# Even shares of FFN pieces, single GpSimd products and stores on SyncE in an RWKV and SwiGLU kernel

## The chip, the cores and the metric

The kernel runs on one core of one Trainium2 chip. The metric is the device time of one execution in microseconds (us), lower being better. The kernel before took 592.2 us (the median of 3 runs, 592.04 to 593.37). A core has five engines, each with an instruction queue of its own that it works through in order: TensorE (PE in the profile, PEld its weight loads), VectorE (DVE), ScalarE (ACT), GpSimd (POOL) and SyncE (SP, which here only starts DMAs; ACT starts some too). Waits between engines go by semaphores.

## The reference

An attention layer (RWKV-5) with 4 batches, 8 heads, 768 positions and head width 48 is followed by a SwiGLU feed-forward block (FFN) over the 3072 rows that it gives:

```python
# per batch and head; w in 0.85 to 0.95, u small
for t in range(S):
    cur = outer(u * k[t], v[t])
    y[t] = r[t] @ (state + cur)
    state = w[:, None] * state + outer(k[t], v[t])
x = y.transpose(0, 2, 1, 3).reshape(B * S, H * D)      # 3072 x 384
g, val = x @ w_gate, x @ w_val                         # 384 x 1536 each
out = (g / (1 + exp(-g)) * val) @ w_out                # 1536 x 384
```

All is 32-bit floating point, apart from the weights, which come as 64-bit numbers and are rounded in the kernel.

## The kernel before, in words

**Attention in 24 steps.** The sequence is cut into 24 blocks of 128 rows; step `s` of the main loop (`for s in range(4, N + 2)`; steps 0 to 3 are written out before it, the head) prepares block `s + 1`, makes the scores of block `s - 1` and the outputs of block `s - 2`. From block 12 (`PAIRED`) a block is two halves of 64 rows from two batches. Per block GpSimd makes four products of 128x384: `scale_k` (k times a table of powers of w, L353), `scale_r` (r likewise, L356), and in `own_product` `own_begin` (r times k, L264) and `own_end` (times u, L267). DVE sums the last by rows at the start of the step of that block (`own_sum`, L275); ACT makes eight diagonals from the sums (`diagonal`, L376, through the queue `small`). SP moves the scaled products in blocks (`move_blocks`, L435, eight DMAs), DVE transposes them in the next step (`turn_blocks`, L456). `paired_scores` lets TensorE make the scores (L523) and, beside them, the state update of the block before (L571). What DVE does with both goes into the queue `lazy`: four masked copies (L531) and four state adds (L587), and with the second add of each half GpSimd multiplies the state by w^64 (L590, with the table `w64`). Before the next scores are made, what is left in `lazy` is flushed.

**The FFN in pieces.** The gate, value and output matmuls are cut into pieces, closures in the list `todo`. `queue(g)` adds them at odd steps: 24 gate pieces for the first pair of blocks, then groups of 41, 40 and 40 pieces at steps 9, 13 and 17, and 13 at step 21. A group has projection pieces (`two_projections`, L740), and 26 pieces of `three_beside`, which hold 60 rounds of matmuls: a round is four instructions of L924. A fast algorithm for 3x3 blocks is used there, for which GpSimd adds up weight tiles (`w_forms`, L854, nine per group of fifteen rounds) and, in the first of these groups alone, weights in place (`in_place`, L827); DVE and ACT add up results out of PSUM (L948) and ACT and DVE make the activation (L955, L948).

**The order.** All is written out by hand. `gaps(s, n)` is called at five places of a step (n = 0 to 4) and takes pieces from `todo` by `feed`. Each piece that is fed takes one item of `lazy` along, and up to three of `small`. At n = 0 a step computes its share of pieces, which is spread over the five gaps; one of gap 1's is fed inside `turn_blocks`. Up to step 17 the share empties `todo` by the step before the next group comes (at most 14 pieces a step); from step 18 it divides what is queued, and 14 to come, by the steps left:

```python
if s < 18:
    share[0] = min(-(-len(todo) // (4 - (s - 9) % 4)), 14)
else:
    share[0] = -(-(len(todo) + (14 if s < 21 else 0)) // max(25 - s, 1))
```

At the start of a step `scale_k`, `scale_r` and `own_product` of the next block are issued one after the other, then the loads of block `s + 3`. In even steps from 10 on (`late`), `scale_r` and the loads come later, behind gap 1.

**The tail.** After step 25 the last eight blocks go through `three_units` (60 rounds, L924) and `project_thirds` (the output matmuls, L1153), twice. `store` (L1118) starts the DMAs of the finished rows: on ACT, but in the second of the two projections, for the first block of each pair, on SP. A block is two pieces of 64 rows, so two DMAs. In the first of the two projections that is eight DMAs on ACT, in the second four on each queue.

**w^64.** GpSimd raises w to the 64th power by six products of 128x4 (L1421) in step 9; ACT copies each half of the partitions into `w64` (L1426) and SP sends it to the other half (L1427). The head makes on DVE a table `pw` with w^(128 - x) in column x.

Of the kernel before, what the change touches and what calls it, by code (L numbers as in the profile page):

```python
# [22 lines left out]
def fast(  # L23
# [112 lines left out]
    def pieces_of(i):  # L136

        if i < PAIRED:
            c, b = divmod(i, B)
            return [(slice(0, P), b, P * c)]  # L140
        return [(slice(64 * p, 64 * p + 64), *part(i, p)) for p in range(2)]
# [127 lines left out]
    def own_product(i):  # L269
        own_begin(i)  # L270
        own_end(i)
# [83 lines left out]
    def scale_r(i):  # L355
        pool.tensor_mul(rhat_of(i)[:, :, 0:D], raw(i)[1], rscale)  # L356
# [6 lines left out]
    def keep_natural_tables():  # L363
        for bank, dst in zip(banks, (kscale, rscale)):
            act.copy(dst, bank[:].rearrange("p (h x) -> p h x", h=H)[:, :, 0:D])
# [96 lines left out]
    def scores(i):  # L462

        ps = [next_psum(HP, P) for _ in range(2)]
        if i >= PAIRED:
            paired_scores(i, ps)
            return
        for a in range(HP):
            for e in range(2):
                rows = slice(64 * e, 64 * e + D)  # L470
                pe.matmul(  # L471
                    ps[e][:, a, :], kT[i % 2][rows, at(i, a), :], turned[i][rows, at(i, a), :],
                    start=True, stop=True, skip_group_check=True,
                )

        def masked_copy(e):
            dst = At[i % 2][:].rearrange("p (a e) t -> p a e t", e=2)[:, :, e]
            m = mask[:, 0].bitcast(INT32).unsqueeze(1).to_broadcast([P, HP, P])
            dve.copy_predicated(dst, m, ps[e][:])

        for e in range(2):
            lazy.append(lambda e=e: masked_copy(e))
        lazy.popleft()()
        if i < BLOCKS:
            lazy.popleft()()
# [596 lines left out]
    def project_thirds(g):  # L1082
# [29 lines left out]
        open_ = {}  # L1112

        def store(q, j):
            issue = sp if ends and j == 0 else act
            for x, b, t in pieces_of(2 * (g + q) + j):
                n0 = S * b + t
                issue.dma_start(  # L1118
                    out=out[n0 : n0 + x.stop - x.start, :],
                    in_=rows[x, q, DM * j : DM * j + DM],  # L1120
                )
# [147 lines left out]
    def feed(n, pops=1):  # L1269
        for _ in range(n):  # L1270
            ready = [k for k, (need, _) in enumerate(todo) if need <= done["pool"] + len(summed)]
            if ready:
                todo.pop(ready[0])[1]()
            if lazy:
                lazy.popleft()()
            for _ in range(min(pops, len(small))):
                small.popleft()()
# [22 lines left out]
    def gaps(s, n):  # L1300

        if s not in EARLY:
            if n == 0:
                if s < 18:
                    share[0] = min(-(-len(todo) // (4 - (s - 9) % 4)), 14)
                else:
                    share[0] = -(-(len(todo) + (14 if s < 21 else 0)) // max(25 - s, 1))
            feed(
                share[0] // 5 + (n < share[0] % 5) - (n == 1 and BLOCKS <= s < N),
                3 if s >= PAIRED else 1,  # L1310
            )
            return
        for what in EARLY[s][n]:
            if what == "R":
                if done["pool"] < NW:
                    round_weights()
                elif len(summed) < 4:
                    weight_sum()
            else:
                feed(1, 3)  # L1320
# [31 lines left out]
    flush()  # L1352
    round_high(1, 0, 1)
    keep_natural_tables()
    scores(1)
    round_dve(0, 0)
    add_low(0, 0)
# [54 lines left out]
    for s in range(4, N + 2):  # L1412
        if 4 < s < N:
            own_sum(s)
        if PAIRED <= s < N:
            diagonal(s)
        late = BLOCKS < s + 1 < N and s % 2 == 0
        if s + 3 == PAIRED:

            for _ in range(6):  # L1420
                pool.tensor_mul(bad, held[:] if _ == 0 else bad, held[:] if _ == 0 else bad)  # L1421
            for e in range(2):
                rows, o = slice(64 * e, 64 * e + 64), 64 - 64 * e
                act.copy(mask64[rows], mask[rows, 0, 64 * e : 64 * e + 64])
                act.copy(ident64[rows], ident[rows, 64 * e : 64 * e + 64])
                act.copy(w64[rows, :, e], bad[rows])  # L1426
                sp.dma_start(out=w64[rows, :, 1 - e], in_=bad[o : o + 64])  # L1427
        if s + 1 == BLOCKS:
            turn(s)
        if s + 1 < N:  # L1430
            scale_k(s + 1)
            if not late:
                scale_r(s + 1)
            own_product(s + 1)
            if s + 1 < BLOCKS:
                load_v(s + 1)
            if s + 3 < N and not late:
                load(s + 3)
        if s + 1 < BLOCKS:
            turn(s)  # L1440
        gaps(s, 0)
        if s > N:
            outputs(s - 2)
        if 4 <= s - 1 < N:
            flush()
            while lazy:
                lazy.popleft()()
            if s - 2 >= PAIRED:
                outputs(s - 2)
                if s < N:  # L1450
                    fill_own(s)
            scores(s - 1)
            if LATE <= s < PAIRED + 2:
                outputs(s - 2)
                update(s - 2)
                fill_own(s)
            if PAIRED <= s < N:
                load_v(s)
            gaps(s, 1)
        if BLOCKS <= s < N:  # L1460
            turn_blocks(s)
        if PAIRED <= s < N:
            fill_turned(s)
        if late:
            scale_r(s + 1)
        if s + 2 == PAIRED:
            sp.dma_start(out=scales[64:P, 1:3], in_=scales[0:64, 1:3])
        if BLOCKS <= s + 1 < N:
            move_blocks(s + 1)
            if s + 1 < PAIRED:  # L1470
                load_v(s + 1)
        if late and s + 3 < N:
            load(s + 3)
        gaps(s, 2)
        if 4 <= s - 2 < LATE - 2:
            outputs(s - 2)
            update(s - 2)
        if s >= 5 and s % 2:
            queue((s - 3) // 2)
        if s < PAIRED:  # L1480
            diagonal(s)
        if s - 2 >= 4:
            gaps(s, 3)
        gaps(s, 4)
        if s == 12:

            dve.tensor_tensor(bad, held[:], wcol[:], ALU.not_equal)
            dve.tensor_reduce(badc, bad, axis=AX.X, op=ALU.add)
            dve.memset(ones, 1.0)
            n_ps = next_psum(HP, P)  # L1490
            pe.matmul(n_ps[0:1, 0, 0:1], badc, ones, start=True, stop=True)
            act.copy(outside, n_ps[0:1, 0, 0:1])
# [435 lines left out]
```

## Time and profile before

| | |
|---|---|
| runs | 593.37, 592.20, 592.04 us; median 592.2 |
| the profiled execution | 592.9 us |
| its span (first to last instruction) | 591.1 us |
| mean granted clock of TensorE | 0.995 |
| busy: PE, PEld | 572.7 us (97%), 513.3 us (87%) |
| busy: DVE, POOL, ACT | 443.8 us (75%), 364.3 us (62%), 223.2 us (38%) |
| chain of work that ended last | PE 75%, POOL 10%, DVE 7%, SP's queue 2% |

How to read it: "busy" is the time in which an engine's instructions ran; for TensorE the ends are modelled. A row of the timeline has start, duration, engine, line, operation, written tile, read tiles, sizes, count, and in brackets how long the engine was idle before it and whom the profile takes for the releaser. The releaser is inferred: where the engine named had long been done, it was another. A row of the waits has waiter, whom it waited for, total us, times, and the longest. The granted clock is the share of its full speed at which TensorE was let run. Steps are found by their first instruction on DVE, the row sum L275.

### The profile page before, as it was taken

Reading aid. Unit: us, or ns where it says so; the run is one execution under the profiler, and the core shown is the slowest. Engines: PE = TensorE matmul, PEld = TensorE weight load, DVE = VectorE, ACT = ScalarE, POOL = GpSimd, SP = SyncE. Lnnn points to the kernel's source line nnn. Section 1 sums busy time; section 2 is a strip of 40 time slices with the busy share of each in tenths; the row PEclk is TensorE's granted clock in tenths of the full one; section 3 lists DMA queues with packets and bytes.
Section 4 is the critical chain, followed back from the end, with each engine's and each line's share of the span. In section 5 each row is a group of like instructions: output and inputs, shape, how many; then the busy total and the mean of one; then the engine's idle time right before and its main releaser. Section 6 shows DMA issues by size and latency. Waiting matters only on the chain.

```text
span 591.1 us, 13539 instructions
## 1 busy us (share of the span) xinstructions
PE 572.7 (97%) x5370; PEld 513.3 (87%) x5370; DVE 443.8 (75%) x761; ACT 223.2 (38%) x529; POOL 364.3 (62%) x382
## 2 busy tenths in 40 slices
PE   7999999999999899999999999999999999999996
PEld 6778888899888799887899987889988899888896
DVE  7978787479579869588689777979557877377672
ACT  4658886341353321345231343431134320233410
POOL 6889888989999403978340998414878960011610
PEclk9999999999999999999899999999999999999999
DMA  7998977544643313335335354320200000200002
GB/s 192 234 247 243 291 214 79 95 69 90 126 84 64 65 33 81 87 53 110 68 63 112 96 97 75 58 46 7 53 2 1 0 1 2 54 0 1 1 3 56
DMA packets 151734, 48.09 MB, mean 81 GB/s; under 512 B 139313, under 2 KB 142386, under 8 KB 151666
## 3 DMA queue, kind: packets, MB, share of 16 engines
q1 hardware_dynamic: 146418, 39.71, 32.2%
q10 hardware_dynamic: 5248, 7.47, 4.5%
q8 instruction: 43, 0.70, 0.5%
q14 instruction: 25, 0.20, 0.1%
HBM read 28.31 MB, written 4.72 MB: 56 GB/s over the span
## 4 chain that ended last, share of the span: by engine, by line
PE 75%; POOL 10%; DVE 7%; SPq 2%; issue 2%; ACT 1%; DMA 1%; ACTq 1%; DVEq 0%; POOLq 0%
PE bank L924 23%; PE ring L924 12%; PE bank L740 12%; PE bank L665 11%; PE bank L1153 8%; POOL s L854 4%; POOL wgv L827 3%; DVE hv L948 3%; PE ring L622 2%; PE ring L557 2%; PE ring L471 1%; PE ring L1153 1%; PE ring L523 1%; PE ring L405 1%; SPq L153 1%
## 5 line engine op out<-in xcount | busy, mean ns | idle before, releaser
L948 DVE TENSOR_TENSOR hv<-hv,bank 128x512 f32<-128x512 f32 x132 | 86.6, 683 | 33.7 <-PE bank L924 25.8
L924 PE MATMUL bank<-xf,wgv 128*128 128x256 f32 x256 | 66.9, 386 | 0.0
L590 POOL TENSOR_TENSOR v_ld<-v_ld,w 48x384 f32<-48x384 f32 x20 | 19.3, 965 | 76.8 <-DVE v_ld L587 75.1
L665 PE MATMUL bank<-xT,wgv 128*128 128x256 f32 x288 | 66.2, 384 | 0.0
L948 ACT COPY hv<-bank 128x512 f32<-128x512 f32 x72 | 40.3, 588 | 68.3 <-PE bank L924 52.3
L665 PEld LDWEIGHTS bank<-xT,wgv 128*128 128x128 f32 x288 | 53.4, 190 | 8.0
L924 PEld LDWEIGHTS bank<-xf,wgv 128*128 128x128 f32 x256 | 48.3, 192 | 7.0 <-DVE kT L1198 0.6
L1207 POOL TENSOR_TENSOR hv<-At,hats 128x512 f32<-128x512 f32 x8 | 10.2, 1273 | 66.6 <-ACT At L1206 66.6
L955 ACT ACTIVATE hv<-hv 128x512 f32<-128x512 f32 (+1 forms) x33 | 21.2, 669 | 51.2 <-DVE hv L948 48.8
L924 PE MATMUL bank<-xT,s 128*128 128x256 f32 x152 | 36.1, 382 | 3.9 <-ACT hv L948 2.6
L924 PE MATMUL bank<-xT,wgv 128*128 128x256 f32 x144 | 36.0, 383 | 0.8 <-DVE hv L948 0.8
L924 PEld LDWEIGHTS bank<-xT,s 128*128 128x128 f32 x152 | 28.4, 190 | 9.6 <-issue 3.7
L740 PE MATMUL bank<-wo,hs 128*128 128x192 f32 x192 | 34.0, 327 | 0.3 <-DVE hv L756 0.2
L854 POOL TENSOR_TENSOR s<-wgv 128x256 f32<-128x256 f32 x39 | 29.6, 780 | 7.6 <-PE bank L740 7.5
L740 PE MATMUL bank<-wt,hs 128*128 128x192 f32 x192 | 33.7, 328 | 0.1
L740 PE MATMUL bank<-wo,hv 128*128 128x192 f32 x192 | 33.4, 327 | 0.0
L740 PEld LDWEIGHTS bank<-wo,hs 128*128 128x128 f32 x192 | 31.6, 190 | 1.1 <-DVE hv L756 0.4
L740 PEld LDWEIGHTS bank<-wt,hs 128*128 128x128 f32 x192 | 31.3, 190 | 0.7 <-issue 0.6
L740 PEld LDWEIGHTS bank<-wo,hv 128*128 128x128 f32 x192 | 31.6, 190 | 0.4
L854 POOL TENSOR_TENSOR s<-s,wgv 128x256 f32<-128x256 f32 x39 | 29.7, 761 | 2.5
L924 PEld LDWEIGHTS bank<-xT,wgv 128*128 128x128 f32 x144 | 26.7, 190 | 5.0 <-DVE hv L948 1.6
L854 POOL TENSOR_TENSOR s<-s 128x256 f32<-128x256 f32 x39 | 29.9, 767 | 0.8
(239 smaller groups left out, 1420.9 us busy)
## 6 DMA issues: line engine op xcount, KB each, us to landing
hats<-hats SPq DMA_DIRECT2D x96, 64.0 KB, 2.3
w_bits<-in_moe_w_gate_dram SPq DMA_DIRECT2D x6, 768.0 KB, 6.3
w_bits<-in_moe_w_val_dram SPq DMA_DIRECT2D x6, 768.0 KB, 6.2
w_bits<-in_moe_w_out_dram SPq DMA_DIRECT2D x6, 768.0 KB, 6.9
At<-zs ACTq DMA_DIRECT2D x24, 128.0 KB, 2.7
At<-rT SPq DMA_DIRECT2D x24, 128.0 KB, 2.4
v_ld<-in_v_dram SPq DMA_DIRECT2D x24, 96.0 KB, 5.8
k_ld<-in_k_dram SPq DMA_DIRECT2D x24, 96.0 KB, 3.1
```

The lines of the kernel that those rows point to most:

```text
L557: pe.matmul(ps[32 * q : 32 * q + 32, cc, 64 * p : 64 * p + 64], *x, start=start, stop=stop, skip_group_check=True,)
L590: pool.tensor_mul(ze, ze, w.unsqueeze(3).to_broadcast([D, HP, 2, D]))
L622: pe.matmul(ps[32 * q : 32 * q + 32, cc, :], *x, start=start, stop=stop, skip_group_check=True,)
L665: pe.matmul(gv[:, o, :].rearrange("p (i t) -> p i t", i=2), wt[:, c, P * f : P * (f + 1)], xT[:, 2 * g % NX : 2 * g % NX + 2, c, :], start ...
L740: pe.matmul(ps, lhs[:, f, :], rhs[:, f, :], start=(f == 0 and n in (0, 1, 4)), stop=(f == FH - 1), skip_group_check=True,)
L827: lambda o=o, x=x, op=op: op(o, o, x) for o, x, op in ((w[1][1], w[0][1], pool.tensor_add), (w[1][1], w[1][2], pool.tensor_sub), (w[0][0], ...
L854: op(made[o], made[a], made[b])
L924: pe.matmul(ps[:, o], u[:, o], v, start=first and o == 0, stop=True, skip_group_check=True,)
L948: do(out, *(pair_of(wide[a][:]) if isinstance(a, str) else a for a in args))
L955: todo.append((at, lambda: act.activation(gate, gate, AF.Silu)))
L1153: pe.matmul(ps, (h[what][q] if h[what] is D_ else h[what][:, q])[:, f, :], wide["o"][what][:, f, :], start=first and f == 0 and (split or ...
L1207: todo.append((muls, lambda: on.tensor_mul(h, sg, value)))
```

## The change

Four things are changed.

1. From step 12 on the share of a step counts all pieces that are still to come (`coming`) and divides by the steps left. And `feed` takes two items of `lazy` along while more than six are waiting.
2. From step 12 (`LATE`) on, GpSimd's products of the next block are no longer issued together: `scale_k` stays at the start of the step, `scale_r` comes behind gap 1 in every step, `own_begin` behind gap 2 and `own_end` behind gap 3. The loads of block `s + 3` come behind `own_begin`.
3. In the tail the first projections' stores are started by SP alone; of the last four pairs of stores, those for the second block of a pair go one on SP and one on ACT.
4. `w64` is copied by ACT from column 64 of `pw` in the head, in place of the six products.

```diff
         def store(q, j):
-            issue = sp if ends and j == 0 else act
-            for x, b, t in pieces_of(2 * (g + q) + j):
+            for p, (x, b, t) in enumerate(pieces_of(2 * (g + q) + j)):
                 n0 = S * b + t
-                issue.dma_start(
+                (act if ends and j and p else sp).dma_start(
...
-            if lazy:
+            for _ in range(min(len(lazy), 1 + (len(lazy) > 6))):
                 lazy.popleft()()
...
             if n == 0:
-                if s < 18:
-                    share[0] = min(-(-len(todo) // (4 - (s - 9) % 4)), 14)
-                else:
-                    share[0] = -(-(len(todo) + (14 if s < 21 else 0)) // max(25 - s, 1))
+                coming = 40 * ((s < 14) + (s < 18)) + 14 * (s < 22)
+                share[0] = -(-(len(todo) + coming) // max(25 - s, 1))
...
     keep_natural_tables()
+    for e in range(2):
+        rows = slice(64 * e, 64 * e + 64)
+        act.copy(w64[rows, :, e : e + 1], pw[rows, :, 64:65])
     scores(1)
...
-            for _ in range(6):
-                pool.tensor_mul(bad, held[:] if _ == 0 else bad, held[:] if _ == 0 else bad)
...
-                act.copy(w64[rows, :, e], bad[rows])
-                sp.dma_start(out=w64[rows, :, 1 - e], in_=bad[o : o + 64])
+                sp.dma_start(out=w64[rows, :, 1 - e], in_=w64[o : o + 64, :, 1 - e])
...
             scale_k(s + 1)
-            if not late:
-                scale_r(s + 1)
-            own_product(s + 1)
-            if s + 1 < BLOCKS:
-                load_v(s + 1)
-            if s + 3 < N and not late:
-                load(s + 3)
+            if s < LATE:
+                if not late:
+                    scale_r(s + 1)
+                own_product(s + 1)
+                if s + 1 < BLOCKS:
+                    load_v(s + 1)
+                if s + 3 < N and not late:
+                    load(s + 3)
...
-        if late:
+        if late or LATE <= s < N - 1:
             scale_r(s + 1)
...
-        if late and s + 3 < N:
+        if late and s < LATE and s + 3 < N:
             load(s + 3)
         gaps(s, 2)
+        if LATE <= s < N - 1:
+            own_begin(s + 1)
+            if s + 3 < N:
+                load(s + 3)
...
         if s - 2 >= 4:
             gaps(s, 3)
+        if LATE <= s < N - 1:
+            own_end(s + 1)
         gaps(s, 4)
```

## The prediction

> **What bounds the kernel now.** I read the head of the page first, then the busy time in windows of 10 us, then every idle gap of TensorE in the timeline, and for each gap the timelines of the engines named in it.
>
> ```profile
> span 591.1 us, 13539 instructions
> PE 572.7 (97%) x5370; PEld 513.3 (87%) x5370; DVE 443.8 (75%) x761; ACT 223.2 (38%) x529; POOL 364.3 (62%) x382
> ...
> 190.00:200.00 10.00, 8.04 (x36) 6.74 (x36) 9.42 (x13) 2.75 (x5) 7.30 (x9) 1.00 0.46 76
> ...
> 280.00:290.00 10.00, 8.92 (x89) 7.79 (x90) 5.68 (x12) 1.42 (x4) 3.54 (x6) 0.83 0.31 58
> ...
> 290.00:300.00 10.00, 9.88 (x47) 8.34 (x46) 9.17 (x16) 4.54 (x8) 2.66 (x3) 1.00 0.50 84
> ...
> 370.00:380.00 10.00, 9.90 (x46) 8.36 (x45) 9.59 (x17) 3.38 (x7) 4.53 (x6) 1.00 0.46 79
> ...
> 274.50 0.55 DVE L275 TENSOR_REDUCE du<-rk 128x8 f32<-128x384 f32 x1
> 359.48 0.55 DVE L275 TENSOR_REDUCE du<-rk 128x8 f32<-128x384 f32 x1
> ```
>
> TensorE is busy 572.7 of 591.1 us, so 18.4 us of idle time is nearly all that a change of order can win. In a window's row stand its length, TensorE's busy time, that of the other engines and, third from the end, the granted clock. Each step begins with DVE's row sum (L275): the two rows are those of steps 18 and 22, which carry ten pieces each, and in the windows behind them (290 to 300, 370 to 380) TensorE is idle for 0.12 and 0.10 us of ten. So ten pieces to a step is a pace that this kernel already runs almost without gaps. The gaps that the change can reach are these (TensorE's timeline; in brackets the idle time and its releaser):
>
> ```profile
> 185.41 1.97 PE L924 MATMUL bank<-xT,s 128*128 128x256 f32 x8 [0.39 <-POOL s L854]
> 190.15 1.99 PE L924 MATMUL bank<-xT,wgv 128*128 128x256 f32 x8 [0.18 <-DVE hv L948]
> 200.78 2.83 PE L924 MATMUL bank<-xT,s 128*128 128x256 f32 x12 [2.60 <-ACT hv L948]
> 281.08 0.62 PE L523 MATMUL ring<-rT,kT 48*64 48x64 f32 x26 [1.66 <-DVE v_ld L587]
> 360.69 1.99 PE L924 MATMUL bank<-xT,wgv 128*128 128x256 f32 x8 [0.59 <-DVE hv L948]
> 364.71 0.62 PE L523 MATMUL ring<-rT,kT 48*64 48x64 f32 x26 [0.73 <-DVE v_ld L587]
> 511.91 1.13 PE L924 MATMUL bank<-xT,s 128*128 128x256 f32 x4 [0.74 <-ACT kT L1198]
> ```
>
> They add up to 6.89 us. The first three lie in step 14, which carries 14 pieces; the fourth at the end of step 17, which carries 4; the next two around the end of step 21, which carries 6; the last in the tail.
>
> **The even shares.** Step 12 starts with 38 pieces queued: in TensorE's order 24 gate pieces and 3 projections stand before it. Before, the formula gives steps 12 to 24 the shares 14, 6, 14, 14, 14, 4, 10, 10, 10, 6, 10, 10, 9. The new one adds the pieces still to come (40 at step 13, 40 at 17, 14 at 21) and divides by 25 - s: ceil(132/13) = 11, ceil(121/12) = 11, then 10 for steps 14 to 23, and 9. TensorE's work is the same. From step 22 on the two orders are equal.
>
> What the short steps cost is seen at 281 us. Scores put eight DVE operations into the lazy queue, four masked copies and then four state adds, one of which goes out with each piece; what is left is flushed just before the next scores. Step 17 and the first gap of step 18 have five pieces, so all four adds run in a row ahead of the scores, which need them:
>
> ```profile
> 279.55 1.48 DVE L587 TENSOR_TENSOR v_ld<-ring,v_ld 48x192 f32<-48x192 f32 x4
> ```
>
> With ten pieces between two scores, and two pops while more than six wait, the eight are out after seven pieces, three pieces ahead of the scores. The stall of 1.66 us goes, and so does what follows it:
>
> ```profile
> 282.00:283.00 1.00, 1.00 (x23) 0.91 (x20) 0.00 (x0) 0.00 (x0) 1.00 (x2) 0.50 0.76 185
> ...
> 281.49 0.29 PE L571 MATMUL ring<-v_ld,hats 64*64 64x48 f32 x2
> 285.58 1.03 PE L924 MATMUL bank<-sgs,wgv 128*128 128x256 f32 x4
> ...
> 348.04 0.63 PE L571 MATMUL ring<-v_ld,hats 64*64 64x48 f32 x32
> 349.57 1.03 PE L924 MATMUL bank<-sgs,wgv 128*128 128x256 f32 x4
> 350.43 1.03 PE L924 MATMUL bank<-xf,wgv 128*128 128x256 f32 x4
> ```
>
> After the gap the granted clock is 0.50, and from the state products to the third round after them TensorE takes 285.58 - 281.49 = 4.09 us, against 350.43 - 348.04 = 2.39 us for the same work four steps later: 1.70 us more. So this place is worth 1.66 + 1.70 = 3.36 us. The 2.60 us gap at 200 us cost no clock (the window of 190 to 200 shows 1.00). [...]
>
> At the end of step 21 the same queue is cut short (six pieces), and DVE is late with an eviction just before: 0.59 + 0.73 = 1.32 us, which I let go with the share of ten, since the windows quoted for ten pieces have 0.1 us. If the cover failed, the 1.32 us would stay.
>
> **GpSimd's products singly.** The largest gap has its cause on two engines:
>
> ```profile
> 195.97 3.99 DVE L948 TENSOR_TENSOR hv<-hv 128x512 f32<-128x512 f32 x1 [0.39 <-ACT hv L955]
> 204.01 0.68 DVE L948 TENSOR_TENSOR hv<-hv 128x512 f32<-128x512 f32 x1
> ...
> 195.73 0.82 POOL L590 TENSOR_TENSOR v_ld<-v_ld,w 48x384 f32<-48x384 f32 x1 [1.26 <-PE bank L924]
> 196.51 0.99 POOL L353 TENSOR_TENSOR hats<-k_ld,scales 128x384 f32<-128x384 f32 x1
> 197.47 0.99 POOL L356 TENSOR_TENSOR hats<-r_ld,scales 128x384 f32<-128x384 f32 x1
> 198.43 0.99 POOL L264 TENSOR_TENSOR rk<-r_ld,k_ld 128x384 f32<-128x384 f32 x1
> 199.49 1.33 POOL L267 TENSOR_TENSOR rk<-rk,scales 128x384 f32<-128x384 f32 x1
> ```
>
> A DVE product with both inputs in SBUF takes 0.68 us alone and 3.99 us here. GpSimd's operations overlap by 0.03 us at each seam until L267, which reads L264's result and leaves 0.07 us; DVE ends 0.47 us after L267's start, and L267 is 0.34 us longer than L264. So DVE was kept out through four operations and got in at the first seam that was open. ACT's copy waits for DVE and TensorE for ACT: 2.60 us. After the change the k product stands at the step's start, the r product behind gap 1, r times k behind gap 2 and the last behind gap 3, two pieces apart each, so GpSimd no longer has four to run in a row. I take the 2.60 us as gone; the bounds are 0 (another seam keeps DVE out as long) and 2.60. The two small gaps at 185 and 190 us (0.57 us) come in a stretch where DVE is behind and GpSimd just as loaded as after; I leave them standing, bounds 0 and 0.57.
>
> [...]
>
> What is moved with them: the r products of odd steps now come behind gap 1, so the eight block moves on SP's queue start later, but they are read a whole step (some 23 us) on; even steps do this already. The loads of step s+3 wait on SP for the product r times k, and behind them queue the next step's v loads. SP waits for that product today too:
>
> ```profile
> SPq L147 <- POOL rk L264: 40.6, 10, 10.2
> ...
> 168.23 0.56 DVE L275 TENSOR_REDUCE du<-rk 128x8 f32<-128x384 f32 x1
> 172.09 1.46 POOL L353 TENSOR_TENSOR hats<-k_ld,scales 128x384 f32<-128x384 f32 x1
> ```
>
> None of the gaps above is released by a load, so I cost this at nothing; without cover it would be the wait itself.
>
> The new wait is DVE's row sum (L275). Its product now ends two pieces before it, where it had a step. Behind it on DVE queue the evictions, and ACT's eight diagonals wait for it. L353 stands right behind L275 in the program, so the two rows show that GpSimd is 172.09 - 168.23 = 3.86 us behind DVE at step 14. A round is 350.43 - 349.57 = 0.86 us, a piece 57/23 rounds or 2.13 us, two pieces 4.26 us. The wait is then 3.86 + 1.0 (L264's 0.99) - 4.26 = 0.6 us, once, as this is the stretch where GpSimd also reworks weights in place. I take 0.6 us; bounds 0 (DVE has idle time that absorbs it) and 0.6 at each of the eleven steps, 6.6 us.
>
> **w^64 and the tail's stores.** Two copies of 64 x 4 move on ACT from step 9 to the head, and GpSimd's six small products go:
>
> ```profile
> 87.56 0.20 ACT L1426 COPY w<-counts 64x4 f32<-64x4 f32 x1
> 15.57 0.48 ACT L626 COPY xT<-ring 128x384 f32<-128x384 f32 x1 [0.23 <-PE ring L622]
> ```
>
> In the head 2 x 0.20 = 0.40 us stand in front of a copy that had 0.23 us to spare, so I take +0.2 us; bounds 0 and 0.4, no gain being possible from added work. At step 9 a DMA on SP no longer waits for the six products; none of TensorE's gaps lies there, so 0, and that cannot turn into a loss.
>
> ```profile
> 505.56 3.08 ACTq L1118 DMA_DIRECT2D out_dram<-hv  x4
> 508.71 2.52 ACTq L1118 DMA_DIRECT2D out_dram<-hv  x4
> 511.27 0.59 ACT L1198 COPY kT<-bank 128x512 f32<-128x512 f32 x1 [2.00 <-PE ring L924]
> ...
> SPq L1118 <- DVE hv L1148: 184.9, 2, 182.4
> ```
>
> Eight store starts keep ACT for 3.08 + 2.52 us, its copy begins at 511.27, and TensorE waits 0.74 us for that. SP has nothing else to do for 182 us, so the starts cost nothing there, and the 0.74 us goes; nothing else is late at that point, as DVE waits for TensorE. At the very end SP issues three stores of a group and ACT one, instead of two each:
>
> ```profile
> L1118 ACTq DMA_DIRECT2D out_dram<-hv x12: 473/618/1279, 505.6 to 586.8; - x12
> L1118 SPq DMA_DIRECT2D out_dram<-hv x4: 466/552/660, 581.9 to 585.9; - x4
> ```
>
> SP's second start ends at 585.9 + 0.66 = 586.6, so its third begins only 0.2 us before the 586.8 of today's last. I take 0, bounds -0.2 and +0.2.
>
> **The sum.** Gone: 3.36 + 1.32 + 2.60 + 0.74 = 8.02 us. Added: 0.6 + 0.2. Net 7.2 us. The profiled execution took 592.9 us (span 591.1 and 1.8 around it), so 585.7; the median of the runs shown is 592.2, 0.7 lower, so **585.0 us**.
>
> **Rivals.**
> (a) Spacing the products does not free DVE: it is shut out as long by the other GpSimd operations, or the four were never worse than single ones and the gap has another cause. For it: in that stretch GpSimd runs back to back, so products issued apart still run without a pause. Against it: the seams. The 2.60 us stays: 587.6 us. Chance 0.17. [...]
> (b) The clock's fall is not the gap's doing: a half-rate stretch of its own comes at some other place. For it: a longer gap at 200 us cost no clock. Against it: it begins right behind the 1.66 us and nowhere else between 120 and 430 us. The 1.70 us stays: 586.7 us. Chance 0.05. [...]
> (c) The uneven shares were not the cause of the gaps in steps 17 and 21, and similar ones come at other steps: only 2.60 and 0.74 go, less 0.8: 589.7 us. Against it are the gapless windows. Chance 0.09.
> (d) Slower: DVE blocks at the row sum. It decides where GpSimd is more than 4.26 - 1.0 = 3.3 us behind DVE two pieces ahead of a step. If the products, now queued behind more forms, are twice as late (7.7 us), DVE stands for 4.4 us in each of the six steps 13, 14, 17, 18, 21 and 22 that make forms. If half of this reaches TensorE, 13 us are added to 585.0 - 0.6: 597.6 us. Against it: the 3.86 us were measured in the stretch with the work in place, which comes once. Chance 0.05.
> (e) The wait of 0.6 us comes at all eleven steps: 585.0 + 6.0 = 591.0, within what a measurement can tell from no change (0.3%, 1.8 us). Chance 0.06.
>
> The forecast has the remaining 0.58. Faster: 0.58 + 0.17 + 0.05 + 0.09 = 0.89; the same: (e), 0.06; slower: (d), 0.05. The range: everything listed gone, with 0.57 more and nothing added, is 8.6 us and with 0.2 from the end 583.4; idle time that I have not listed may add some tenths: 583.0. Above it takes in (b) and (a), the latter with the wait of 0.6 us at two steps more, 588.8; (c), (d) and (e), 0.20 together, are left out.
>
> **What would show it.** Right: no gap of TensorE above 0.6 us between 120 and 430 us; the granted clock 1.00 in every window there; state adds (L587 before) spread one by one and ended before the scores; no DVE product of 0.68 us stretched beyond 2 us; ACT free of store starts near 505 us; TensorE's busy time unchanged but for the 1.7 us. Wrong: a DVE row sum that waits for GpSimd's last product, with evictions late behind it; TensorE released by ACT or DVE for microseconds in steps 13 to 15; a load named as the releaser.

## The result: slower, and the profile after

The changed kernel took 599.25 us (median of 4 runs, 598.01 to 601.09) against 592.5 us for the kernel before (median of 4 runs, one more than the table above has): 1.0115 times as long, 95% interval 1.0085 to 1.0144. It is slower by 6.8 us, or 1.15%, where 7.2 us less had been forecast. The profiled execution took 601.09 us, the longest of the four. Its page begins so:

```profile
span 599.3 us, 13566 instructions
PE 575.3 (96%) x5370; PEld 514.1 (86%) x5370; DVE 448.8 (75%) x761; ACT 222.2 (37%) x529; POOL 365.5 (61%) x376
```

The idle gaps of TensorE in the timeline of the changed kernel, between 170 and 330 us (all above 0.5 us):

```profile
175.45 1.99 PE L924 MATMUL bank<-xT,wgv 128*128 128x256 f32 x8 [1.11 <-DVE hv L948]
...
202.69 4.51 PE L924 MATMUL bank<-xT,s 128*128 128x256 f32 x12 [2.60 <-ACT hv L948]
222.10 2.19 PE L740 MATMUL bank<-wt,hs 128*128 128x192 f32 x12 [0.68 <-DVE hs L714]
227.19 2.22 PE L740 MATMUL bank<-wo,hs 128*128 128x192 f32 x12 [0.96 <-DVE hv L748]
259.71 1.99 PE L924 MATMUL bank<-xT,wgv 128*128 128x256 f32 x8 [0.57 <-DVE hv L948]
...
299.25 4.35 PE L924 MATMUL bank<-xT,s 128*128 128x256 f32 x12 [2.60 <-ACT hv L948]
318.49 2.19 PE L740 MATMUL bank<-wt,hs 128*128 128x192 f32 x12 [0.68 <-DVE hs L714]
323.58 2.22 PE L740 MATMUL bank<-wo,hs 128*128 128x192 f32 x12 [0.96 <-DVE hv L748]
```

The 1.66 us at 281 us, the 0.59 and 0.73 us at the end of step 21 and the 0.74 us in the tail are gone, as forecast. But the 2.60 us stands where it stood, and comes a second time 97 us later; both times the twelve matmuls behind it take 4.51 or 4.35 us where the same twelve took 2.83 before: the clock fell. The waits for DVE's h sums (L714) and additions (L748), 0.68 and 0.96 us, are new, and they come again after 96 us too.

The windows show the same. Both answers below are of the changed kernel: first ten-microsecond windows, then the whole stretch from 120 to 440 us; the third from the end is the granted clock.

```profile
190.00:200.00 10.00, 9.55 (x44) 7.81 (x42) 9.40 (x14) 2.87 (x6) 6.93 (x8) 1.00 0.50 80
200.00:210.00 10.00, 7.40 (x144) 6.02 (x144) 5.60 (x7) 4.05 (x12) 1.32 (x2) 0.83 0.01 2
...
290.00:300.00 10.00, 7.40 (x33) 6.19 (x32) 9.36 (x12) 4.05 (x9) 6.75 (x7) 0.95 0.32 54
...
120.00:440.00 320.00, 306.21 (x3064) 275.05 (x3063) 250.12 (x403) 102.43 (x259) 206.38 (x235) 0.99 0.36 70
```

The same stretch of the kernel before:

```profile
120.00:440.00 320.00, 313.08 (x3106) 282.35 (x3105) 251.60 (x412) 105.80 (x262) 209.74 (x240) 0.99 0.36 71
```

TensorE is idle for 320 - 306.21 = 13.79 us there, against 6.92 before. With two falls of the clock instead of one (1.7 us each) and 0.74 less in the tail that is 6.87 + 1.7 - 0.74 = 7.8 of the 8.2 us by which the span grew. This compares the two profiled executions. How often the clock falls differs between executions of one kernel (the mean granted clock of the kernel before ran from 0.989 to 0.999), so the 1.7 us need not be in the 6.8 us between the medians.

What stands behind the first 2.60 us, in the timelines of DVE and GpSimd of the changed kernel:

```profile
197.13 0.36 DVE L587 TENSOR_TENSOR v_ld<-ring,v_ld 48x192 f32<-48x192 f32 x1
197.88 3.99 DVE L948 TENSOR_TENSOR hv<-hv 128x512 f32<-128x512 f32 x1 [0.39 <-ACT hv L955]
...
197.64 0.83 POOL L590 TENSOR_TENSOR v_ld<-v_ld,w 48x384 f32<-48x384 f32 x1 [0.29 <-PE bank L924]
198.43 1.00 POOL L353 TENSOR_TENSOR hats<-k_ld,scales 128x384 f32<-128x384 f32 x1
199.38 0.99 POOL L356 TENSOR_TENSOR hats<-r_ld,scales 128x384 f32<-128x384 f32 x1
200.34 0.99 POOL L264 TENSOR_TENSOR rk<-r_ld,k_ld 128x384 f32<-128x384 f32 x1
```

It is the picture of before: DVE's product of two SBUF tensors takes 3.99 us instead of 0.68. The three products are two pieces apart in the program, and still they run back to back, with seams that overlap. L590 starts 0.15 us after the state add (L587) that it needs; the three products behind it need only loaded data, and the pieces between which they stand give GpSimd nothing to do here, so nothing holds them apart.

Two rows of the waits show the rest: DVE now waits for GpSimd at the row sum, which it did not before, and of the tail's stores only two are left to ACT (groups by line).

```profile
DVE du L275 <- POOL rk L267: 15.5, 4, 5.4
```

```profile
L1117 SPq DMA_DIRECT2D out_dram<-hv x14: 466/572/1382, 514.6 to 594.8; - x14
L1117 ACTq DMA_DIRECT2D out_dram<-hv x2: 474/480/487, 591.0 to 594.5; - x2
```

### The profile page after: what moved, and what is told of

Same layout as the page of the kernel before. It is cut to its first block, busy times and chain, and to the rows that moved or that the text cites. A ratio compares the mean times of both kernels' runs of the same rounds, so it can differ in the third digit from the quotient of the medians.

```text
span 599.3 us, 13566 instructions
## 1 busy us (share of the span) xinstructions
PE 575.3 (96%) x5370; PEld 514.1 (86%) x5370; DVE 448.8 (75%) x761; ACT 222.2 (37%) x529; POOL 365.5 (61%) x376
## 4 chain that ended last, share of the span: by engine, by line
PE 68%; DVE 16%; POOL 8%; DMA 3%; ACT 2%; issue 2%; SPq 0%; DVEq 0%; ACTq 0%; POOLq 0%
PE bank L924 18%; PE ring L924 13%; PE bank L665 10%; PE bank L740 9%; PE bank L1152 8%; DVE hv L948 6%; POOL s L854 3%; POOL wgv L827 2%; PE ring L622 2%; DVE At L531 2%; PE ring L557 2%; DMA v_ld<-in_v_dram 2%; PE ring L471 1%; DMA At<-zs 1%; PE ring L1152 1%
## 5 line engine op out<-in xcount | busy, mean ns | idle before, releaser
L948 DVE TENSOR_TENSOR hv<-hv,bank 128x512 f32<-128x512 f32 x132 | 86.9, 685 | 32.0 <-PE bank L924 23.3
L590 POOL TENSOR_TENSOR v_ld<-v_ld,w 48x384 f32<-48x384 f32 x20 | 20.5, 1024 | 76.8 <-DVE v_ld L587 71.7
L948 ACT COPY hv<-bank 128x512 f32<-128x512 f32 x72 | 40.3, 587 | 68.7 <-PE bank L924 52.0
L924 PE MATMUL bank<-xf,wgv 128*128 128x256 f32 x256 | 65.7, 381 | 0.0
L924 PE MATMUL bank<-xT,s 128*128 128x256 f32 x152 | 39.2, 407 | 6.2 <-ACT hv L948 5.2
L924 PEld LDWEIGHTS bank<-xT,s 128*128 128x128 f32 x152 | 30.7, 205 | 12.7 <-issue 6.5
L376 ACT ACTIVATE zs<-mask,du 128x64 f32<-128x64 f32 x96 | 25.5, 341 | 29.9 <-DVE du L275 19.4
```

Source lines behind the costliest of these rows:

```text
L376: lambda h=h: act.activation(own[:, i % 2, slot(i, h), :], ident64, AF.Identity, scale=du[:, h : h + 1])
L590: pool.tensor_mul(ze, ze, w.unsqueeze(3).to_broadcast([D, HP, 2, D]))
L924: pe.matmul(ps[:, o], u[:, o], v, start=first and o == 0, stop=True, skip_group_check=True,)
L948: do(out, *(pair_of(wide[a][:]) if isinstance(a, str) else a for a in args))
```

## The experiments

Three reasons offered themselves: the products placed singly (rows at L275 and the run of GpSimd operations), the even shares (the same collision every four steps), the doubled release of `lazy` (the new waits at the projections). Each run's ratio is to the kernel before, timed on the same chip; the medians of before there lay between 591.9 and 594.1 us, so that microseconds of runs from different chips compare to about 2 us only, and the ratios are the safer guide.

| run | median us | ratio, 95% interval |
|---|---|---|
| the changed kernel | 599.25 | 1.0115 (1.0085 to 1.0144) |
| s_alone: even shares alone | 585.40 | 0.9869 (0.9844 to 0.9894) |
| p_alone: products singly alone | 600.15 | 1.0118 (1.0088 to 1.0149) |
| l_alone: doubled release alone | 591.26 | 0.9968 (0.9951 to 0.9985) |
| t_alone: stores and w64 alone | 592.28 | 0.9977 (0.9958 to 0.9996) |
| without_products | 598.68 | 1.0073 (1.0049 to 1.0097) |
| single_release | 584.92 | 0.9840 (0.9819 to 0.9862) |
| own_product_whole | 597.41 | 1.0049 (1.0032 to 1.0066) |
| before_seam | 591.48 | 0.9957 (0.9935 to 0.9979) |
| copies_early | 589.36 | 0.9928 (0.9903 to 0.9954) |
| adds_early | 597.30 | 1.0072 (1.0048 to 1.0096) |
| double_release_seam | 593.91 | 1.0008 (0.9990 to 1.0026) |
| p_alone_whole | 597.91 | 1.0062 (1.0039 to 1.0084) |
| shares_and_stores | 584.41 | 0.9845 (0.9820 to 0.9871) |
| stores_seam | 584.90 | 0.9872 (0.9846 to 0.9898) |

### One part at a time

The even shares alone:

```diff
-                if s < 18:
-                    share[0] = min(-(-len(todo) // (4 - (s - 9) % 4)), 14)
-                else:
-                    share[0] = -(-(len(todo) + (14 if s < 21 else 0)) // max(25 - s, 1))
+                coming = 40 * ((s < 14) + (s < 18)) + 14 * (s < 22)
+                share[0] = -(-(len(todo) + coming) // max(25 - s, 1))
```

> The kernel before with the even shares alone (products, state adds and stores as before). If the repeated collision of the state add's step with the three products is the work of the even shares (steps 15 and 19 at the same place of their group of pieces), TensorE waits 2.60 us for DVE's L948 twice, near 200 and near 300 us, the clock falls after each, the 281-us gap is gone, and the time is 591 to 595 us. If the lone placing of the products is what brings the second 2.60 us, this kernel has it at most once and the time is 588 to 591 us (592.5 less 1.66 and 1.70, plus nothing). No DVE row sum L275 waits for GpSimd in either case.

It took 585.40 us, less than either theory had. There is no 2.60 us at all: the longest wait of TensorE for DVE between 150 and 440 us is 0.37 us (ahead of that stands one of 1.80 us at 147.8 us, to which the best version comes back). GpSimd still runs the four in a row, but DVE's product is through before them (timelines of DVE and GpSimd in the kernel with the even shares alone):

```profile
196.30 0.34 DVE L587 TENSOR_TENSOR v_ld<-ring,v_ld 48x192 f32<-48x192 f32 x1
197.06 0.69 DVE L948 TENSOR_TENSOR hv<-hv 128x512 f32<-128x512 f32 x1 [0.41 <-ACT hv L955]
197.78 0.36 DVE L587 TENSOR_TENSOR v_ld<-ring,v_ld 48x192 f32<-48x192 f32 x1
...
198.28 0.82 POOL L590 TENSOR_TENSOR v_ld<-v_ld,w 48x384 f32<-48x384 f32 x1 [1.86 <-PE bank L924]
199.07 0.99 POOL L353 TENSOR_TENSOR hats<-k_ld,scales 128x384 f32<-128x384 f32 x1
200.02 0.99 POOL L356 TENSOR_TENSOR hats<-r_ld,scales 128x384 f32<-128x384 f32 x1
```

The state add that lets L590 go stands behind the product in DVE's order; in the changed kernel it stands ahead of it. That is one piece's difference.

The products singly alone (the moved `scale_r`, `own_begin`, `own_end` and loads of part 2):

> The kernel before with the products placed singly alone. If placing in program order does not place in time, the row sum L275 waits for GpSimd's L267 for 3 to 6 us in three or four steps, TensorE loses 0.6 to 1.1 us in each of these, the 2.60 us at 200 us stays, and the time is 593 to 597 us. If the products cost only in company with the even shares, the row sum waits under 1 us in all, and the time is within 1.5 us of before's 592.5.

600.15 us, above the first range. A wait of 2.57 us near 200 us stays, and the row sum waits 9.4 us in four places. Two of them reach TensorE; the first, in the timelines of DVE and TensorE:

```profile
171.93 0.55 DVE L275 TENSOR_REDUCE du<-rk 128x8 f32<-128x384 f32 x1 [3.67 <-POOL rk L267]
...
173.22 2.81 PE L924 MATMUL bank<-xT,s 128*128 128x256 f32 x8 [3.81 <-DVE hv L948]
```

The other is 2.75 us of DVE and 2.48 us of TensorE at 284 us: step 17 has four pieces on the old shares, so that nothing stands between `own_end` and the next row sum. At each of the three waits, 3.81, 2.57 and 2.48 us, the clock falls in the profiled execution (0.98 granted over the stretch from 120 to 440 us); the forecast of this run had no falls in it.

The doubled release alone:

```diff
-            if lazy:
+            for _ in range(min(len(lazy), 1 + (len(lazy) > 6))):
                 lazy.popleft()()
```

> The kernel before with the doubled release of state adds alone. If the doubled release is what brings the pairs of waits for DVE's h sums and o additions (0.68 and 0.96 us at 222 and 318 us, 0.69 and 0.69 at 410 us in the changed kernel), these come here too, 1.3 to 1.7 us in each of three groups, the 0.59 and 0.73 us at step 21 go, and the time is 594 to 597 us. If the shares or the products bring them, none of these waits is longer than 0.2 us here, and the time is 591 to 592 us.

591.26 us, in the second range, but not for its reason: the waits that it ruled out are there in part, 0.75 us (L748, 220 us) and a pair of 0.69 and 0.69 us (399 and 404 us), so the doubled release brings waits of this kind on the old shares too. It is no loss here but a small gain, as other waits shrink: the one at 200 us is 0.92 instead of 2.60 us, the one at 281 us 0.95 instead of 1.66 us, and the clock does not fall in the profiled execution (1.00 granted over the stretch from 120 to 440 us). The stores and w64 alone:

> The kernel before with the tail's stores begun by SyncE and w64 from the head's table alone. As reckoned: the 0.74 us near 505 us goes, two copies in the head and five fewer in step 12's preparation move nothing else, 591.5 to 592.2 us. The rival, that these too shift GpSimd's or ACT's timing at step 12 and cost there: a wait of TensorE over 0.5 us that before did not have between 150 and 200 us, and 592.5 us or more.

592.28 us, at the edge of the expected range. The ratio of 0.9977 is 1.4 us less (0.2 to 2.5), which agrees with the 0.74 us reckoned; that wait is gone.

So none of the four parts costs alone what the changed kernel loses, apart from the products, on the old shares.

### One part undone

The changed kernel with the products where before had them, and, in the second, with the old release:

```diff
-            for _ in range(min(len(lazy), 1 + (len(lazy) > 6))):
+            if lazy:
                 lazy.popleft()()
```

> The changed kernel with the products where before had them (even shares, doubled release, end stores and w64 stay). If the single placing of the products is the whole loss, the gain of the even shares comes out: 583.5 to 586 us, no row sum L275 waits for GpSimd, and no wait of TensorE over 1 us between 150 and 440 us. If the doubled release costs at the projections once the shares are even (the 0.68 and 0.96 us pairs at 222 and 318 us and the 0.69 us pair at 410 us of the changed kernel stay), the time is 4 to 5 us above that, 588 to 590 us.

> The changed kernel with the state adds released one a piece, as before had them (products singly, even shares, end stores and w64 stay). If the doubled release brings the three pairs of waits at the projections, they go, 4.3 us less, 594 to 596 us, with both 2.60 us and the waits of L275 still there. If the pairs are the products' doing, they stay and the time is 598 to 601 us.

Both fell outside every expectation, and they settle the part. Without the products 598.68 us: the two waits of 2.58 and 2.59 us, both falls of the clock (0.99 granted from 120 to 440 us) and the 0.69 and 0.57 us are still there. With the single release 584.92 us: all are gone (1.00 granted). The doubled release costs 14.3 us on even shares, with the products (599.25 against 584.92) as without them (598.68 against 584.41, below), and the products themselves next to nothing. This is so although with the single release DVE stands still for the row sum for 15.0 us, six times. The longest such wait, and the only gap of TensorE above 0.25 us between 120 and 440 us (kernel with single release):

```profile
243.08 0.55 DVE L275 TENSOR_REDUCE du<-rk 128x8 f32<-128x384 f32 x1 [4.86 <-POOL rk L267]
...
175.52 1.99 PE L924 MATMUL bank<-xT,wgv 128*128 128x256 f32 x8 [1.10 <-DVE hv L948]
```

4.86 us of DVE cost nothing at 243 us: no matmul result was late for it, and after one short addition DVE even waits 1.52 us for TensorE. 0.89 us at 174 us, the start of step 14, cost TensorE 1.10.

`own_end` right behind `own_begin`, in the changed kernel and in the one with the products alone:

```diff
         if LATE <= s < N - 1:
-            own_begin(s + 1)
+            own_product(s + 1)
...
-        if LATE <= s < N - 1:
-            own_end(s + 1)
```

> The changed kernel with own_end right behind own_begin after the third run of pieces, not one run of pieces later. If the waits of the row sum L275 for L267 are the larger part of what the products cost, they fall from 15.5 us to under 5 us, the 1.11, 0.57 and 0.57 us of TensorE go, and with less held up behind them the time is 594 to 597 us. If DVE is shut out whatever the place of own_end, the two 2.60 us stay and move, and the time is within 2 us of the changed kernel's 599 us.

> The kernel before with the products placed singly, but own_end right behind own_begin. If the row sum's wait for L267 is what the single products cost on the old shares (3.81 and 2.48 us of TensorE and a fall of the clock behind each), these go and the time is 590 to 594 us. If it is the shut-out by a run of GpSimd operations at some place, the row sum's waits shrink and the time stays at 597 to 600 us.

In the changed kernel the row sum's waits fell to 7.7 us and the 1.11 us went, but the 0.57 us stayed, and so did 2.21 and 2.59 us: 597.41 us, above the first range and within the second. So the expectation had put the 0.57 us down to the row sum wrongly. On the old shares 597.91 us, not the 590 to 594 hoped for; it lies in the second range, but there is no shut-out on TensorE's path of the old size, since the wait at 201 us is 0.74. The row sum still waits twice, and TensorE's gap follows it in size. In the timelines of DVE and TensorE:

```profile
170.25 0.55 DVE L275 TENSOR_REDUCE du<-rk 128x8 f32<-128x384 f32 x1 [1.51 <-POOL rk L267]
...
171.55 1.75 PE L924 MATMUL bank<-xT,s 128*128 128x256 f32 x7 [1.50 <-DVE hv L948]
```

Against 3.67 and 3.81 us above: there the row sum's wait is TensorE's. What brings further waits of 1.63 us (232 us) and 1.89 us (285 us) in that kernel was not tried, so what the single products cost on the old shares is explained in part only.

### What in the doubled release costs

It sends the first two masked copies out with one piece, so that all that follows, copies and state adds, comes one piece earlier. Two kernels part this. In the first the copies come early and one piece then takes nothing along, so that the adds stay in their old places; in the second the copies stay and the last copy and the first add go together.

```diff
-            for _ in range(min(len(lazy), 1 + (len(lazy) > 6))):
+            k = min(len(lazy), 1 + (len(lazy) > 6))
+            if k == 2:
+                ahead_of[0] = True
+            elif ahead_of[0] and len(lazy) == 4:
+                k, ahead_of[0] = 0, False
+            for _ in range(k):
                 lazy.popleft()()
```

```diff
-            for _ in range(min(len(lazy), 1 + (len(lazy) > 6))):
+            if len(lazy) > 6:
+                whole[0] = True
+            k = min(len(lazy), 1)
+            if whole[0] and len(lazy) == 5:
+                k, whole[0] = 2, False
+            for _ in range(k):
                 lazy.popleft()()
```

> The changed kernel, whose doubled release is kept for the masked copies and made up for by one piece that takes nothing along before the four state adds, so that the adds go with the same pieces as in the run with single release. If what the doubled release costs is the place of the state adds (both halves' adds ahead of DVE's product L948, so that GpSimd's L590 and the three products run in a row against it), the 2.60 us at 200 and 300 us and the pairs at the projections go, and the time is that of single release, 584 to 587 us. If two copies at once right behind the scores are the cause, all of it stays: 595 to 600 us.

> The changed kernel with the extra release moved: the masked copies go one a piece as with single release, the last copy and the first state add go together, so that the four adds keep the early places that the doubled release gives them. It is the counterpart of the run copies_early. If the place of the adds is worth about 10 us and the copies the rest (589.4 against 584.9), this kernel has the two 2.60 us with the falls of the clock, has not the 0.69 us at the first h sums (216 and 307 us) nor the 0.57 us, and takes 593.5 to 596.5 us. If the two are not separate, because any operation put ahead on DVE costs the same, the 0.69 and 0.57 us stay and the time is that of the changed kernel, 598 to 601 us.

Early copies alone: 589.36 us, between the two expectations and 4.4 above single release. No 2.60 us, no fall of the clock (1.00 granted from 120 to 440 us), but the waits of 0.69 us at 216 and 0.57 us at 253 us stay. The first of them, in the timelines of DVE and TensorE:

```profile
206.99 0.89 DVE L531 COPY_PREDICATED At<-mask,ring 64x256 f32<-64x256 int32 x2
...
215.16 0.96 DVE L714 TENSOR_TENSOR hs<-hs,hv 128x768 f32<-128x768 f32 x1
...
216.26 2.19 PE L740 MATMUL bank<-wt,hs 128*128 128x192 f32 x12 [0.69 <-DVE hs L714]
```

And with the single release:

```profile
207.03 0.43 DVE L531 COPY_PREDICATED At<-mask,ring 64x256 f32<-64x256 int32 x1
...
214.55 0.96 DVE L714 TENSOR_TENSOR hs<-hs,hv 128x768 f32<-128x768 f32 x1
215.54 0.44 DVE L531 COPY_PREDICATED At<-mask,ring 64x256 f32<-64x256 int32 x1
```

Two copies run at 207 us in place of one, and so one copy of 0.44 us that had stood behind the h sum is now ahead of it. The projections begin at 211.51 and 211.56 us, so the two kernels are in step until then; the sum begins 0.61 us later, and TensorE waits 0.69 us for it.

Early adds alone: 597.30 us, 12.4 above single release and somewhat above what was expected. The 0.69 and 0.57 us are gone, both waits of 2.59 us are there, and the wait for L748 has grown to 1.41 us. From TensorE's timeline:

```profile
202.88 2.83 PE L924 MATMUL bank<-xT,s 128*128 128x256 f32 x12 [2.59 <-ACT hv L948]
225.50 2.22 PE L740 MATMUL bank<-wo,hs 128*128 128x192 f32 x12 [1.41 <-DVE hv L748]
296.49 4.51 PE L924 MATMUL bank<-xT,s 128*128 128x256 f32 x12 [2.59 <-ACT hv L948]
```

So the adds are the larger part and the copies the smaller; 4.4 and 12.4 are more than the 14.3 of both. Probably a copy that goes early is also out of the way of a later wait: the one for L748 is 1.41 us with early adds alone and 0.96 us with both. This was not tried by itself.

### The seam

GpSimd's order within the run of four, with nothing else changed: in the kernel before, in the one without the products, and in the best one.

```diff
+            own_product(s + 1)
             scale_k(s + 1)
             if not late:
                 scale_r(s + 1)
-            own_product(s + 1)
```

> The kernel before with the two own products ahead of the scales of k and r in the issue order of a step, nothing else. Near 200 us GpSimd then runs L590, L264, L267, L353, and L267 needs what L264 makes, so there is a seam after the second operation and not after the fourth. If DVE gets SBUF at a seam, its L948 of 3.99 us shortens to about 2.2 us, TensorE's 2.60 us to about 0.8 us, the clock stays, and the time is 589 to 591 us. If DVE is shut out by any four in a row, seam or not, the 3.99 and the 2.60 us stay and the time is 592 to 593.5 us.

> The kernel of the run without the products (even shares, doubled release, products together as before), with the two own products issued ahead of the two scales. It should open a seam after the second of GpSimd's operations in a row, near 200 and near 296 us. If the two shut-outs and the two falls of the clock behind them are the larger part of what the doubled release costs, each 2.60 us becomes about 0.7, the clock stays at 1.00, and the time falls from 598.7 by 2 x (1.9 + 1.7) = 7.2 to about 591.5 us. If the waits at the projections are the larger part, or if a wait of 0.7 us is enough for a fall of the clock, the time stays above 594 us.

The kernel before with the seam took 591.48 us, half a microsecond above the first range and below the second (timelines of DVE, GpSimd and TensorE):

```profile
196.77 2.08 DVE L948 TENSOR_TENSOR hv<-hv 128x512 f32<-128x512 f32 x1 [0.39 <-ACT hv L955]
...
197.31 0.99 POOL L264 TENSOR_TENSOR rk<-r_ld,k_ld 128x384 f32<-128x384 f32 x1
198.38 1.33 POOL L267 TENSOR_TENSOR rk<-rk,scales 128x384 f32<-128x384 f32 x1
...
199.67 2.83 PE L924 MATMUL bank<-xT,s 128*128 128x256 f32 x12 [0.69 <-ACT hv L948]
```

The same instructions in another order, and 3.99 us become 2.08, 2.60 become 0.69: DVE gets in where L267 has to wait for what L264 makes. That it is this wait, and not L267 as such, shows in the kernel with the products singly alone. There L267 stands second in the run too, but L264 had ended 2.9 us before, no seam opens, and DVE is kept out again:

```profile
200.47 3.89 DVE L948 TENSOR_TENSOR hv<-hv 128x512 f32<-128x512 f32 x1 [0.49 <-ACT hv L955]
...
200.13 0.82 POOL L590 TENSOR_TENSOR v_ld<-v_ld,w 48x384 f32<-48x384 f32 x1 [0.83 <-PE bank L924]
200.91 1.00 POOL L267 TENSOR_TENSOR rk<-rk,scales 128x384 f32<-128x384 f32 x1
201.87 0.99 POOL L353 TENSOR_TENSOR hats<-k_ld,scales 128x384 f32<-128x384 f32 x1
```

On the doubled release both 2.6 us become 0.7 and neither fall of the clock comes (the twelve matmuls at 201 us take 2.83 us instead of 4.51; mean granted clock of the profiled execution 0.997 instead of 0.990): 593.91 instead of 598.68 us, 4.8 of the 7.2 us expected.

### The version that beats both

> The kernel before with the even shares, the end stores and w64 from the head's table, without the doubled release and without the single products. If the single products are worth nothing on even shares, and the parts add up, this is the run with even shares alone less the 1.06 us of TensorE at 504 us: 584 to 585 us, at or below the run with single release (584.9). If the single products bring something there, it is 1 us or more above that run: 586 us or more.

> Even shares, end stores and w64 alone (584.4 us), with the own products issued ahead of the scales. If with even shares and single release no shut-out is left on TensorE's path, the seam is worth nothing there: 583.5 to 585.5 us. If the remaining waits of TensorE for DVE (0.38 us at 264 us and its like at 354 us) came from runs of GpSimd operations, they go: 583 to 583.6 us. If the earlier own products hold up the block moves, 586 us or more.

Even shares, end stores and w64 alone take 584.41 us, 1.55% less than before and 14.8 us less than the changed kernel. Over the stretch from 120 to 440 us TensorE is idle for 2.81 us:

```profile
120.00:440.00 320.00, 317.19 (x3140) 287.20 (x3139) 257.01 (x418) 107.87 (x269) 221.27 (x248) 1.00 0.36 70
```

The seam adds nothing to it (584.90 us), because no shut-out is left on TensorE's path. The single products add nothing either: with them it is the run with single release, 584.92 us. But that is a balance of two waits. Without the products 1.80 of the 2.81 us are one wait, for three small operations of DVE in step 12 (L1484 to L1486):

```profile
147.55 0.19 PE L1488 MATMUL ring<-counts 128*1 128x1 f32 x2 [1.80 <-DVE counts L1486]
```

With the products it is gone, and the 1.10 us at 175 us stands in its place. Why it is gone was not tried.

## Why the prediction was wrong, step by step

- **The step that failed** is in the even shares: "With ten pieces between two scores, and two pops while more than six wait, the eight are out after seven pieces, three pieces ahead of the scores." The count is right, but the doubled pop was put into the sum at nothing. Which of DVE's operations the released ones come ahead of was not looked at. One piece earlier puts the state add ahead of DVE's product L948, so that GpSimd's L590 and the products behind it run against that product (2.6 us and a fall of the clock, twice in the profiled execution), and copies and adds ahead of the h sums and additions that TensorE waits for. In all 14.3 us (599.25 less 584.92). Without that release the changed kernel takes 584.92 us, where 585.0 had been forecast, but so close a hit is partly luck: the kernel before took 594.1 us on that chip, so 9.2 us went and not 7.2, and the 2.60 us went for another reason than the one given (below).
- **281 us and step 21** (3.36 + 1.32 us): right but for 0.37 us of the 0.59, which the even shares alone leave (at 355 us); the doubled release was not needed for the rest. The clock did not fall there in the runs with even shares (1.00 granted from 120 to 440 us in s_alone, single_release and shares_and_stores; in the changed kernel it fell at 203 and 299 us alone).
- **The 2.60 us at 200 us**: credited to the wrong part. "GpSimd no longer has four to run in a row" failed in every kernel with the single products: GpSimd has nothing to do or to wait for in the pieces between its products here, and so they run back to back (198.43, 199.38 and 200.34 us in the changed kernel), wherever they stand between the pieces. What removes the 2.60 us is the even shares with the single release, by the order on DVE. That the 2.60 us had no fall of the clock to pay for was luck of the execution that was read: with the stores and w64 alone the same wait, 2.59 us at the same place, is followed by one (the twelve matmuls behind it take 4.51 us). Rival (a) had the outcome, the stay of the 2.60 us, and its reason for it, that products issued apart still run without a pause, is what the trace shows.
- **The reading of the shut-out itself** (DVE kept out through four operations, in at the first open seam) was right: before_seam shows it (2.08 us instead of 3.99).
- **The row sum** (0.6 us, once): at step 14, where it was reckoned, it is 0.89 us, and TensorE paid 1.10. In all the wait was under-sized, 15.0 us in six places on even shares, but TensorE paid at this one alone. Rival (d)'s mechanism is there: on the old shares it costs 3.81 and 2.48 us. On even shares with the single release TensorE does not wait at the other five places, so it did not bring the result.
- **Rival (c)**, that uneven shares were not the cause, fell with s_alone. **Rival (b)**, a fall of the clock that is not the gap's doing, has no support: the falls left with the waits in s_alone, single_release and double_release_seam (mean granted clock of the profiled executions 1.000, 0.999 and 0.997, against 0.994 in the changed kernel).
- **The tail** (0.74 us): right. **The two copies in the head** (0.2 us): too small to be told.

## What to carry to other kernels

Moving work earlier in a queue was not free here, it cost 14.3 us: name, for each instruction that moves, the one it now stands ahead of, and ask who waits for that one. Instructions that stand apart in the program need not run apart: three GpSimd products, two pieces apart each, started 0.95 and 0.96 us after one another, as their engine had nothing to do or to wait for between them. Before several parts of a change go in together, time each alone and each left out: here one part alone was worth 8 us, another alone 2 us, and with both (and the stores) the kernel was 4.6 us slower than before.

## What the runs showed of the hardware

- **The same wait was followed by a fall of the clock in one place and not in another.** In the run with early adds the same wait of 2.59 us came twice; behind the first the twelve matmuls took 2.83 us, behind the second 4.51. The clock records in the traces of the kernel before and of the changed kernel have each fall at 3.41 us long (but the last of a run, at the very end) and at half rate. In both the falls begin whole multiples of 3.413 us apart: in the changed kernel the second begins 95.57 us, 28 times that, after the first. Counted from a fall in intervals of this length, the 2.60 us of the kernel before, which cost no clock, are cut in two (1.49 and 1.11 us), and its 1.66 us lie whole in one, at whose end the clock falls; in the changed kernel the first 2.60 us lie whole in one, and of the second 2.27 us do. Between 120 and 440 us of these two traces a fall follows each of these three intervals, with 1.66, 2.60 and 2.27 us of idle time, and none with 1.49 us or less. That the place of a wait in these intervals decides is an estimate from these two traces. It would explain why the same kernel has more falls in one execution than in another (the mean granted clock of the kernel before ran from 0.989 to 0.999).
- **A run of GpSimd operations kept DVE out until one of them waited for the one before.** DVE's product L948 took 3.99 us with four in a row, 2.08 with the dependent pair as second and third, shown by order alone, and 0.68 alone. The products that were stretched had both inputs in SBUF: in the kernel with even shares alone L948 with one input in PSUM kept its 0.69 us beside the same four.
